# Left-over scatters placed behind the last weight split, and both halves of the last store issued by SP, in an attention, convolution and mixture-of-experts kernel

## The chip, the cores and the metric

The kernel runs on one core of one Trainium2 chip. The metric is the device time of one execution in microseconds (us). A TensorE, VectorE, ScalarE, GpSimd and SyncE instruction stands in the profile under PE (PEld for its weight loads), DVE, ACT, POOL and SP. The clock of TensorE has two levels, 2.4 and 1.2 GHz, which the profile shows as a granted clock of 1.0 and 0.5.

## The reference, cut to what matters

The inputs are q, k, v of 8 batches, 8 heads, 256 positions and 64 values a head, a gate of 8 x 256 x 512, a convolution of 15 taps for each of 512 channels, and 16 experts in 4 groups with weights of 512 x 1024 and 1024 x 512.

```
scores = q @ k.T / 8;  attn = softmax(scores);  x = attn @ v          # [8, 256, 512]
c = depthwise_conv(x * sigmoid(gate), conv_w);  x = x + c * sigmoid(c)
x = x.reshape(2048, 512)
g = argmax(x @ w_group);  e = argmax(x @ w_expert[g])                  # for each token
out = softmax(group logits)[g] * softmax(expert logits)[e] * (relu(x @ w1[g, e]) @ w2[g, e])
```

## The kernel before

**Stages.** The 2048 tokens are 16 tiles of 128, two for each of the 8 batches. Attention, convolution and routing run in four groups of two batches. The expert stage is split in two. The *dense* part (`dense`) takes each batch as a whole, finds the one expert that most of its 256 tokens chose, loads that expert's weights once and multiplies all 256 tokens with them; results of tokens that chose another expert are replaced afterwards or, for the loop at the end, recomputed. The *left-over* part (`leftover`) gathers tokens of the first six batches that chose another expert into three tiles of 32 rows, computes these with their own experts, and scatters the rows over the output with indirect DMAs that GpSimd issues (`spread`, which calls `scatter`, line 1297). A loop at the end (lines 1392 to 1404) handles further left-over tiles; its trip count is read on the chip, and with these inputs the profile shows the branch past it and no work of its body.

**Weights.** An expert's weights are 8 tiles of 128 x 1024 float32 (512 KB each): tiles 0 to 3 are the first layer, 4 to 7 the second. Every tile goes through `fetch` (SP issues its load, line 934) and `split`: ACT rounds the tile to `wh` (line 323, by way of `copy`), and then two halves of 512 columns give `wl` = raw - `wh` (line 957), most on POOL. For the last two batches all `wl` halves are on POOL. TensorE multiplies high with high, high with low and low with high parts, so it needs `wh` and `wl` of a tile: lines 984 for the first layer, 1019 to 1021 and, for the second 128 tokens of the last batch, 1010 to 1012 for the second layer. Two rings tie the steps together: 4 buffers `raw` (a fetch waits until POOL has split the tile four before it) and 4 pairs `wh`, `wl` (a cast waits until TensorE has used the tile four before it). I number the 64 tiles 0 to 63 over the batches; 56 to 63 belong to the last batch, `ms[-1]`. Hidden values go the same way: ACT makes `hh` (line 1032), DVE or, for tile 58, ACT and POOL make `hl` (lines 1041, 1038 and 1045).

**Order.** The order of instructions on each engine's queue is set when the program is built. A planner (`Flow`) runs all steps as coroutines over estimated durations: `yield run(engine, us)` queues a step, and of the steps that are ready on an engine the one with the lowest key goes next. Weight splits have key -1 and `spread` has key 50, so a scatter is placed where POOL has no other ready step in the plan; `fl.sc` keeps the three of them 2.3 us apart in the plan. `yield flag(f)` holds a step until another has set `f`. `m.st` are the flags of a batch's two stores, `m.w` those of its 8 split tiles. On the chip each queue then runs in that fixed order with semaphore waits. All scatters write the same rows, so each waits for the one before it to have landed.

**The end.** The last tile of 128 tokens is computed in two halves of 256 columns, and `half` scales each (DVE the first at line 1057, ACT the second at line 1055) and stores it (line 1060), the first from SP, the second from ACT. The 128 tokens before them are stored by `store` (line 1074).

Of the kernel before, what the change touches and what calls it, by code (L numbers as in the profile page):

```python
# [17 lines left out]
P = 128  # L18
# [70 lines left out]
class Flow:  # L89
# [169 lines left out]
    def run(self):  # L259
        while True:  # L260
            best = None
            for e, q in self.q.items():
                if q:
                    t = max(self.free[e], min(x[2] for x in q))
                    if best is None or t < best[0]:
                        best = t, e
            if best is None:
                return
            t, e = best
            if e == "PE":  # L270
                x = min((x for x in self.q[e] if x[2] <= t), key=lambda x: (x[0] + SW * (x[6] != self.shape), x[1]))
            else:
                x = min((x for x in self.q[e] if x[2] <= t), key=lambda x: x[:2])
            self.q[e].remove(x)
            k = x[4]
            k[2], k[3], k[4] = self.spot(e, t, x), e, e
            self.free[e] = k[2]
            self.step(k)
# [28 lines left out]
def flag(f):  # L307
    return "flag", f
# [7 lines left out]
def attn_conv_moe(ctx, tc, aQ, aG, cw, wr, wE, cst, out):  # L316
    nc = tc.nc
    v_, a_, g_, t_, s_ = nc.vector, nc.scalar, nc.gpsimd, nc.tensor, nc.sync

    on = dict(DVE=v_, POOL=g_, ACT=a_, SP=s_)  # L320
# [625 lines left out]
    ms = [M(b) for b in range(B)]  # L946
# [15 lines left out]
    def dense():  # L962
        for m in ms:
# [30 lines left out]
            for j in range(4):  # L994
# [5 lines left out]
                for t in range(2):  # L1000
                    sl = slice(t * P, (t + 1) * P)
                    if m.b == B - 1 and t == 1:
                        if j == 3:
                            yield get("y")
                            y = work.tile([P, DM], F32, name="y", bufs=2)
                        for h in range(2):
                            yield run("PE", 0.71)
                            c, yp = slice(h * S, h * S + S), ys[1 + h][:, 0:S]
                            for k in range(2):
                                t_.matmul(yp, hh[:, k, sl], w3h[:, k, c], start=j == 0 and k == 0, stop=False)  # L1010
                                t_.matmul(yp, hh[:, k, sl], w3l[:, k, c], start=False, stop=False)  # L1011
                                t_.matmul(yp, hl[:, k, sl], w3h[:, k, c], start=False, stop=j == 3 and k == 1)  # L1012
                            if j == 3:
                                fl.go(half(m, h, c, y, yp), -5, fl.now[2], "PE")
                        continue
                    for k in range(2):
                        if DC or k == 0:
                            yield run("PE", 0.705 if DC else 1.41)
                        t_.matmul(ys[t], hh[:, k, sl], w3h[:, k, :], start=j == 0 and k == 0, stop=False)  # L1019
                        t_.matmul(ys[t], hh[:, k, sl], w3l[:, k, :], start=False, stop=False)  # L1020
                        t_.matmul(ys[t], hl[:, k, sl], w3h[:, k, :], start=False, stop=j == 3 and k == 1)  # L1021
                    if j == 3:
                        fl.go(store(m, t, iy[t], ys[t]), -5, fl.now[2], "PE")
# [26 lines left out]
    def half(m, h, c, y, yp):  # L1050
        yield flag(gr[m.g].done)
        tt = 2 * m.b + 1
        yield run(("DVE", "ACT")[h], (0.35, 0.33)[h])
        if h:
            a_.activation(y[:, c], yp, AF.Copy, scale=rec[:, tt, 1:2])  # L1055
        else:
            v_.tensor_scalar(y[:, c], yp, rec[:, tt, 1:2], None, ALU.mult)
        w = ("SP", "ACT")[h]
        yield run(w, 0.43)
        on[w].dma_start(out=out[tt * P:(tt + 1) * P, c], in_=y[:, c])  # L1060

    def store(m, t, iy, yp):
        yield flag(gr[m.g].done)
# [232 lines left out]
    def scatter(o, n):  # L1296
        g_.indirect_dma_start(out=out_rows[0:n, :], out_offset=bass.IndirectOffsetOnAxis(ap=o.ix, axis=0),
                              in_=o.ys, in_offset=None, bounds_check=n - 1, oob_is_err=False)
# [51 lines left out]
    def leftover():  # L1350
        for s in range(NS):
            o = ls_[s]
            yield flag(ready[s])
            for h in range(2):
                for j in range(4 * h, 4 * h + 4):
                    yield flag(lraw[s][j])
                    fl.now[2] = max(fl.now[2], o.w[j][2])
                raw = [o.w[j][1] for j in range(4 * h, 4 * h + 4)]
                yield from (o.second(raw) if h else o.first(raw))
                for j in range(4 * h, 4 * h + 4):  # L1360
                    fl.put("gv", o.w[j][0])
            fl.go(spread(o), 50, fl.now[2])

    def spread(o):
        for m in ms[0:GB[GA]]:
            for f in m.st:
                yield flag(f)
        fl.now[2] = max(fl.now[2], fl.sc)
        yield run("POOL", 1.0)
        scatter(o, TA * P * NC)  # L1370
        fl.sc = fl.now[2] + 2.3
# [83 lines left out]
```

## Time and profile before

| | us |
|---|---|
| median of 3 runs | 352.19 |
| range of these runs | 350.96 to 352.76 |
| the profiled execution's own time | 351.07 |
| its span, first to last instruction | 349.3 |
| PE busy | 336.0 (96% of the span) |
| POOL busy | 286.0 (82%) |
| DVE busy | 256.2 (73%) |
| ACT busy | 239.5 (69%) |
| granted TensorE clock, mean | 0.989 |

A line of the timeline gives start and duration in us, the engine (SPq and ACTq: a DMA issued from that queue), the source line, the operation, what is written and read, and how many instructions; in brackets the engine's idle time ahead of it and what ended it. A matmul's end is modelled, so the idle time of PE is best read from one start to the next. A line of a window gives its length, the busy time of each engine with the number of instructions that start in it, the granted clock, the DMA engines' busy share and the GB/s they moved. The view of one source line gives durations as minimum, median and maximum in ns and the first and last start.

### The profile page before, as it was taken

The page shows a single profiled execution, that of the slowest core. Times are in us where ns is not written, and L with a number is a line of the kernel's source. Part 1 is how long each engine was busy: PE and PEld are TensorE (multiplying, and loading weights), DVE is VectorE, ACT ScalarE, POOL GpSimd, SP SyncE. Part 2 cuts the span into 40 slices and gives each one's busy share as a digit, 9 for nine tenths or more (in the row PEclk, how much of TensorE's full clock was granted, in tenths as well). Part 3 has the DMA queues.
Part 4 walks back from the last instruction along what each step waited for, and adds up shares of the span by engine and source line. Part 5 has one row for each costly group of instructions (what it writes and reads, how often), then busy time and mean ns, then how long its engine had stood idle before and what let it go on. Part 6 is the DMA issues. An engine that isn't in the chain of part 4 may idle for free. (4 is left out here: it accounts for less than half of the span.)

```text
span 349.3 us, 7977 instructions
## 1 busy us (share of the span) xinstructions
PE 336.0 (96%) x2749; PEld 272.9 (78%) x2749; DVE 256.2 (73%) x542; ACT 239.5 (69%) x546; POOL 286.0 (82%) x279
## 2 busy tenths in 40 slices
PE   8999999998999999999999999999999999999892
PEld 6766555567788789878877788899789788988872
DVE  1989997999999999999899888997994462101000
ACT  4999578969997797798988955365554535627211
POOL 0652477766999999999999989999899989993990
PEclk9999999999999999999999999999999999999897
DMA  7849896439955681568551545599999847556301
GB/s 252 292 142 270 233 261 213 150 137 341 350 180 202 190 293 62 213 239 269 206 192 68 175 139 224 187 340 391 407 408 410 326 149 266 190 188 176 121 3 66
DMA packets 29883, 77.89 MB, mean 223 GB/s; under 512 B 3230, under 2 KB 3798, under 8 KB 29840
## 3 DMA queue, kind: packets, MB, share of 16 engines
q1 hardware_dynamic: 27520, 73.31, 61.7%
q10 hardware_dynamic: 2160, 3.80, 2.9%
q8 instruction: 24, 0.39, 0.4%
q0 software_dynamic: 160, 0.23, 0.2%
q14 instruction: 19, 0.16, 0.1%
HBM read 65.50 MB, written 7.57 MB: 209 GB/s over the span
## 5 line engine op out<-in xcount | busy, mean ns | idle before, releaser
L957 POOL TENSOR_TENSOR wl<-raw,wh 128x512 fp32r<-128x512 f32 x121 | 156.0, 1318 | 7.6 <-ACT wh L323 3.8
L736 DVE SCALAR_TENSOR_TENSOR bk<-sl,cwq,bk 128x512 f32<-128x512 f32 x151 | 108.7, 747 | 2.2 <-ACT bk L723 0.5
L323 ACT CAST wh<-raw 128x1024 fp32r<-128x1024 f32 x64 | 67.1, 1054 | 29.8 <-DMA raw<-wE 13.0
L984 PE MATMUL bk<-sl,wh 128*128 128x256 f32 x512 | 74.0, 287 | 0.0
L984 PEld LDWEIGHTS bk<-sl,wh 128*128 128x128 f32 x512 | 65.8, 191 | 2.4 <-issue 1.6
L562 ACT ACTIVATE pr<-bk,nm 128x256 f32<-128x256 f32 x128 | 59.1, 487 | 9.8 <-DVE nm L557 9.7
L1019 PE MATMUL bk<-wh,hh 128*128 128x512 f32 x120 | 48.7, 406 | 0.0
L1020 PE MATMUL bk<-wl,hh 128*128 128x512 f32 x120 | 47.5, 396 | 0.7 <-POOL wl L957 0.7
L557 DVE TENSOR_REDUCE nm<-bk 128x2 f32<-128x512 f32 x64 | 40.3, 679 | 9.8 <-PE bk L528 9.7
L1021 PE MATMUL bk<-wh,hl 128*128 128x512 f32 x120 | 47.4, 395 | 0.0
L1041 DVE SCALAR_TENSOR_TENSOR hl<-bk,hh 128x512 fp32r<-128x512 f32 x16 | 11.0, 688 | 49.3 <-ACT hh L1032 42.6
L984 PE MATMUL bk<-sl,wl 128*128 128x256 f32 x256 | 41.4, 285 | 2.0 <-POOL wl L957 2.0
L984 PEld LDWEIGHTS bk<-sl,wl 128*128 128x128 f32 x256 | 35.5, 193 | 2.2 <-POOL wl L957 2.2
L569 PE MATMUL bk<-c_id,pr 128*128 128x128 f32 x256 | 34.9, 277 | 2.1 <-ACT pr L562 1.9
L1032 ACT ACTIVATE hh<-bk 128x512 fp32r<-128x512 f32 x32 | 19.2, 600 | 23.9 <-PE bk L984 16.5
L569 PEld LDWEIGHTS bk<-c_id,pr 128*128 128x128 f32 x256 | 28.0, 141 | 8.9 <-ACT pr L562 5.4
L528 PE MATMUL bk<-qk 64*128 64x256 f32 x256 | 34.3, 404 | 0.2
L548 PE MATMUL bk<-pT,gv 128*64 128x256 f32 x256 | 31.2, 386 | 0.0
L528 PEld LDWEIGHTS bk<-qk 64*128 64x128 f32 x256 | 24.6, 194 | 6.3 <-issue 1.9
L562 ACT ACTIVATION_READ_ACCUMULATOR pr<-bk,nm 128x1 f32 x128 | 28.1, 219 | 0.0
L1020 PEld LDWEIGHTS bk<-wl,hh 128*128 128x128 f32 x120 | 22.6, 188 | 5.6 <-POOL wl L957 1.1
L1021 PEld LDWEIGHTS bk<-wh,hl 128*128 128x128 f32 x120 | 22.6, 188 | 5.3
(176 smaller groups left out, 550.9 us busy)
## 6 DMA issues: line engine op xcount, KB each, us to landing
raw<-wE SPq DMA_DIRECT2D x64, 512.0 KB, 4.3
gv<-wE SPq DMA_DIRECT2D x24, 512.0 KB, 8.8
gv<-aG SPq DMA_DIRECT2D x16, 512.0 KB, 6.6
qk<-aQ SPq DMA_DIRECT2D x15, 512.0 KB, 5.6
out_dram<-y SPq DMA_DIRECT2D x9, 256.0 KB, 3.8
wh<-sl SPq DMA_DIRECT2D x8, 270.0 KB, 4.9
wl<-sl SPq DMA_DIRECT2D x8, 270.0 KB, 5.5
x_rows<-y ACTq DMA_DIRECT2D x8, 256.0 KB, 2.1
```

The source lines that it names most:

```text
L323: (a_.copy if e == "ACT" else on[e].tensor_copy)(o, i)
L528: t_.matmul(scs[hh][:, qt, :], t[sl, i, qt * P:(qt + 1) * P], t[sl, i, 256:512], start=True, stop=True)
L548: t_.matmul(u.a[64 * hh:64 * hh + 64, i, :], u.vt[:, i, kt, hh, :], pTs[hh][1][:, kt, :], start=kt == 0, stop=kt == 1)
L557: v_.reduce_max(nm[:, hh, :], sc, axis=AX.X, negate=True)
L562: a_.activation(pr[:, qt, :], sc[:, qt, :], AF.Exp, bias=nm[:, hh, qt:qt + 1], scale=1.0, accum_out=u.sm[:, i, qt, hh, 0:1])
L569: t_.transpose(tp[:, kt, qt * P:(qt + 1) * P], pr[:, qt, kt * P:(kt + 1) * P], ident)
L736: v_.scalar_tensor_tensor(acc if k == KT - 1 else ac, x, w, acc if k == m and m > 1 else ac, ALU.mult, ALU.add)
L957: on[e].tensor_tensor(wl[:, sl], raw[:, sl], wh[:, sl].bitcast(F32), ALU.subtract)
L984: t_.matmul(hp[:, f, :], ww[:, f, c, :], x, start=k == 0, stop=k == 11)
L1019: t_.matmul(ys[t], hh[:, k, sl], w3h[:, k, :], start=j == 0 and k == 0, stop=False)
L1020: t_.matmul(ys[t], hh[:, k, sl], w3l[:, k, :], start=False, stop=False)
L1021: t_.matmul(ys[t], hl[:, k, sl], w3h[:, k, :], start=False, stop=j == 3 and k == 1)
```

## The change

Two edits. `half` issues the store of both halves from SP, where the second was issued from ACT. `spread`, which places one scatter of left-over rows, waits for the eight splits of the last batch's weights in addition to the stores of the first six batches, so that all three scatters stand behind the last split on POOL's queue.

```diff
@@ half
             a_.activation(y[:, c], yp, AF.Copy, scale=rec[:, tt, 1:2])
         else:
             v_.tensor_scalar(y[:, c], yp, rec[:, tt, 1:2], None, ALU.mult)
-        w = ("SP", "ACT")[h]
-        yield run(w, 0.43)
-        on[w].dma_start(out=out[tt * P:(tt + 1) * P, c], in_=y[:, c])
+        yield run("SP", 0.43)
+        s_.dma_start(out=out[tt * P:(tt + 1) * P, c], in_=y[:, c])
@@ spread
         for m in ms[0:GB[GA]]:
             for f in m.st:
                 yield flag(f)
+        for f in ms[-1].w:
+            yield flag(f)
         fl.now[2] = max(fl.now[2], fl.sc)
         yield run("POOL", 1.0)
         scatter(o, TA * P * NC)
```

## Rows read from the trace of the kernel before

**Rows 1.** Chain that ended last, its two ends: start us, duration us, what

```profile
336.79 1.25 POOL wl L957
...
342.99 0.47 ACT y L1055
```

**Rows 2.** Timeline of PE, last batch: first layer, then second layer

```profile
315.62 1.11 PE L984 MATMUL bk<-sl,wh 128*128 128x256 f32 x8
...
318.46 1.11 PE L984 MATMUL bk<-sl,wh 128*128 128x256 f32 x8
...
321.30 1.11 PE L984 MATMUL bk<-sl,wh 128*128 128x256 f32 x8
324.43 1.22 PE L984 MATMUL bk<-sl,wl 128*128 128x256 f32 x4 [2.02 <-POOL wl L957]
...
330.79 0.40 PE L1019 MATMUL bk<-wh,hh 128*128 128x512 f32 x1
...
336.32 0.39 PE L1019 MATMUL bk<-wh,hh 128*128 128x512 f32 x1
...
337.01 0.40 PE L1019 MATMUL bk<-wh,hh 128*128 128x512 f32 x1
338.08 0.50 PE L1020 MATMUL bk<-wl,hh 128*128 128x512 f32 x1 [0.67 <-POOL wl L957]
338.42 0.39 PE L1021 MATMUL bk<-wh,hl 128*128 128x512 f32 x1
...
342.67 0.28 PE L1012 MATMUL bk<-wh,hl 128*128 128x256 f32 x1
```

**Rows 3.** Windows: length; PE, PEld, DVE, ACT, POOL; clock; DMA share; GB/s

```profile
324.40:327.90 3.50, 3.48 (x16) 3.48 (x17) 0.00 (x0) 0.00 (x0) 3.50 (x3) 0.51 0.02 9
```

**Rows 4.** Timeline of POOL: the three scatters

```profile
315.33 1.03 POOL L1297 DMA_INDIRECT out_dram<-ys,ixs  x1 [0.16 <-issue]
322.10 0.98 POOL L1297 DMA_INDIRECT out_dram<-ys,ixs  x1 [5.73 <-DMA out_dram<-ys,ixs]
...
339.43 0.99 POOL L1297 DMA_INDIRECT out_dram<-ys,ixs  x1 [0.16 <-issue]
```

**Rows 5.** Windows of POOL's outage and of the stretch behind it, columns as before

```profile
315.33:323.08 7.75, 7.07 (x58) 6.77 (x57) 1.38 (x2) 5.43 (x7) 2.02 (x3) 1.00 0.61 167
323.08:339.28 16.20, 14.18 (x88) 12.99 (x89) 0.69 (x1) 3.80 (x5) 16.19 (x13) 0.89 0.21 67
```

**Rows 6.** Line 1297, the three scatters from issue to landing

```profile
DMA to landing us min/median/max: 2.1/2.1/6.5
```

**Rows 7.** Timeline of ACT: casts of tiles 58 to 62 and the `tm` of tile 58

```profile
315.00 1.04 ACT L323 CAST wh<-raw 128x1024 fp32r<-128x1024 f32 x1
...
317.09 2.19 ACT L323 CAST wh<-raw 128x1024 fp32r<-128x1024 f32 x2 [0.47 <-ACT y L1069]
...
322.00 1.04 ACT L323 CAST wh<-raw 128x1024 fp32r<-128x1024 f32 x1
...
328.64 0.59 ACT L1038 ACTIVATE tm<-bk 128x512 f32<-128x512 f32 x1
330.00 1.06 ACT L323 CAST wh<-raw 128x1024 fp32r<-128x1024 f32 x1 [0.77 <-DMA raw<-wE]
```

**Rows 8.** Timeline of SP: the fetches of tiles 62 and 63

```profile
326.84 1.56 SPq L934 DMA_DIRECT2D raw<-wE  x2
```

**Rows 9.** Timeline, line 1060: the stores of the last two halves

```profile
342.82 0.35 SPq L1060 DMA_DIRECT2D out_dram<-y  x1
...
343.49 0.34 ACTq L1060 DMA_DIRECT2D out_dram<-y  x1
```

**Rows 10.** Line 1060: the last half from issue to landing

```profile
DMA to landing us min/median/max: 3.2/3.2/3.2
```

**Rows 11.** Line 1393, branch past the loop on TensorE's queue, from 343 us

```profile
L1393 PEldq COMPARE_BRANCH  x1: 3792/3792/3792, 343.1 to 343.1; - x1
```

**Rows 12.** Line 1074, two stores of 256 KB beside the first scatter: issue to landing

```profile
DMA to landing us min/median/max: 5.7/5.7/5.7
```

## The prediction

> **What bounds the kernel now.** I read the page's busy shares first (PE 96%), then the chain of waits, then the timelines of PE and POOL over the last batch, because both edits lie there. The chain is short [rows 1]: it runs from ACT's scaling of the last half back through TensorE's second layer to one weight split on POOL that ends at 336.79 + 1.25 = 338.04 us. So the end of the kernel hangs on TensorE, and TensorE in turn hung on POOL shortly before. The timeline of PE shows two places where it waited for `wl` [rows 2]: at 324.43 (tile 58) and at 338.08 (tile 62). Around the first the granted clock fell to the lower level: the mean is 0.51 over 324.40 to 327.90, right after TensorE had stood idle [rows 3]. The reason stands in POOL's timeline: scatter one is issued at 315.33, scatter two waits 5.73 us for the first to land and is issued at 322.10 [rows 4]. From 315.33 to 323.08 POOL thus does no split (its 2.02 busy us are the two scatters), and from 323.08 to 339.28 it runs 13 operations without a gap, 16.20 / 13 = 1.246 us each [rows 5]: it is catching up until the last split. Scatter three already stands behind the last split.
>
> **Edit 1, what it takes away on TensorE.** Tiles 56 and 57 take 318.46 - 315.62 = 321.30 - 318.46 = 2.84 us each at full clock. Tiles 58 and 59 at that pace would end at 321.30 + 2 x 2.84 = 326.98; the second layer begins at 330.79 [rows 2]. That is 3.81 us, of which some 2.1 are the stall and the rest matmuls at the low clock [rows 2, 3]. In the second layer three starts take 337.01 - 336.32 = 0.69, so 0.23 each; the matmul due at 337.24 starts at 338.08 (0.84 lost) and the one after it 0.34 later (0.11 lost) [rows 2]. Sum: 3.81 + 0.95 = **4.76 us**, if POOL no longer holds TensorE up.
>
> **Does POOL keep up without the two scatters?** Up to 315.33 its queue is the same. ACT's casts of tiles 58 to 61 end at 316.04, about 318.2, 319.28 and 323.04 [rows 7], and none of them waited for POOL's outage. I take the order of halves that the stretch behind the outage has (two tiles interleaved), which is the less favourable one: half 58a at 316.1, 59a when cast 59 is done at 318.2, then at 1.246 us each 58b, 59b, 60a, 60b up to 324.4, 61a to 325.7, the `hl` of tile 58 to 326.9 (its `tm` at 328.64 - 3.81 = 324.8 to 325.4 [rows 7]), 61b to 328.2. Fetch 62 needs 58b, done at 320.7, so it leaves then instead of at 326.84 [rows 8]. Its landing was seen by ACT at 330.00, 3.2 us after issue [rows 7, 8]; with 6.5 (the scatter's worst [rows 6], taken as a bound) it lands at 327.2 and its cast ends at 328.3, when POOL gets to it. Tile 63's cast has to wait until TensorE is through with tile 59 at 326.98 and ends at 328.1. So 62a, 63a, 62b, 63b run from 328.2 to 333.2, with 62b ready at 331.9. TensorE wants it at 326.98 + (336.32 - 330.79) + 0.92 = 333.43 [rows 2]. The slack is 1.5 us, some 5 us for tile 58 (wanted at 322.4, ready at 317.4). TensorE is then the bound throughout, and its last matmul ends at 342.67 + 0.28 - 4.76 = 338.19 instead of 342.95 [rows 2].
>
> **Edit 1, what it adds.** Three scatters in a row behind the last split, each waiting for the one before. Third and second scatter landed in 2.1 us and the first in 6.5 [rows 6]; from a landing (315.33 + 6.5 = 321.83) to the next issue pass 0.27 us [rows 4]. The DMA engines were 0.61 busy in the window around the first, and 0.21 in the one behind [rows 5]; at the end no fetch is left, so I take 2.1: 333.2 + 0.16 (idle before an issue [rows 4]) + 3 x 2.1 + 2 x 0.27 = 340.2. Bounds: 3 x 2.1 to 3 x 6.5, an end between 340.2 and 353.4. Behind the scatters only POOL's part of the closing waits is queued; no engine needs POOL for data any more. What covers them is the end of the program: TensorE's branch past the loop takes 3.79 us from 343.1 to 346.9 [rows 11], and the last half lands at 343.49 + 3.2 = 346.7 [rows 9, 10]; from there to the span's end at 349.3 pass 2.4 us. Both move 4.76 us forward, to 342.1. The scatters land 1.9 us before that, so they cost nothing; without that cover each us of them is a us of the kernel.
>
> The Trainium skill, "DMA: Bandwidth & Descriptors", section "Latency and other measured facts", puts the fixed cost of a DMA down mostly to the memory's latency, small at light load and up to 2 us at high load. By that the 2.1 us scatters are the quiet case and three of them stay covered; the 6.5 us one in a busy window agrees with it in direction only.
>
> **Edit 2.** SP has finished issuing the first half at 342.82 + 0.35 = 343.17, before ACT ends the second at 342.99 + 0.47 = 343.46 [rows 1, 9], so SP issues it no later than ACT did (343.49). A gain is excluded, since the branch ends at 346.9 and the landing at 346.7: an earlier landing is hidden. A loss is bounded by the landing of two stores beside the first scatter, 5.7 instead of 3.2 [rows 10, 12]: 343.49 + 5.7 = 349.2, 2.3 us past the branch. I take zero: the nearest row is the last half itself.
>
> **The rivals.**
> *Part of the gain is given back* (chance 0.09). One of the three scatters takes 6.5 us: the chain ends at 340.2 + 4.4 = 344.6, 2.5 past the cover, and 4.76 - 2.5 = 2.3 us remain, 349.9. A plan that puts the last splits some 3 us later than I do gives about the same. Against it: tile 62's slack of 1.5 us and the empty DMA engines.
> *The scatters slow the last stores* (0.05). The third scatter now runs beside them, as the first did beside two stores of 256 KB that took 5.7 us [rows 12]. The end moves back 2.3 us: gain 2.4, 349.8. Against it: those stores shared the DMA engines with a weight fetch too.
> In the same section, the Trainium skill says that two of the 16 DMA engines are usually slower and gives GpSimd's descriptor rings as a best guess; by it stores beside scatters would land late, which is this rival. No row here tells it from plain load.
> *Nothing that can be told from no change* (0.08). The outage belongs to this one execution, because scatter one is usually as quick as the others: the outage would be 4.4 us shorter and 4.76 - 4.4 = 0.4 us is left, 351.8. Against it: the profiled execution (351.07) is among the shortest, where it should be the longest. Or the plan orders the last batch otherwise and TensorE finds another wait.
> *Slower* (0.04). The serial chain of three becomes the end. From 333.3 on, each us of mean landing counts three times. It breaks even when the chain ends at the old 346.9, at a mean of (346.9 - 333.3 - 0.5) / 3 = 4.4 us, and is slower by over 0.5% from 4.9. At 6.5 each it ends at 353.4, 6.5 past the old point: 358.7. For it: one of three was that slow. Against it: that one shared the DMA engines with a fetch.
>
> **How the numbers follow.** The profiled execution's own time is 351.07 for a span of 349.3, so 1.8 us lie around the span and stay. It is 1.1 us under the median of the runs; I subtract from the median: 352.19 - 4.76 = **347.4** (346.3 by the profiled execution). Forecast 0.74, and its own range is 345.9 to 348.8: the spread of the runs before is 1.8 us, and TensorE's sum can be off by some half a us. The two rivals that give a part back lie at 349.8 and 349.9, so the range goes to 350.0. A change under 0.5% (1.8 us) can't be told from none here. Faster by more than that: 0.74 + 0.09 + 0.05 = 0.88; within it 0.08; slower 0.04.
>
> **What would show it.** Right: no wait for `wl` on PE in the last batch, clock 1.0 up to the last matmul, the second layer some 3.8 us earlier; POOL without a gap over 1 us between 318 and 333, then three scatters about 2.4 us apart, the last one landed before the branch past the loop is over; both halves' stores on SP. Wrong: a wait of ACT for a fetch or of TensorE for `wl` in tiles 60 to 63, a landing of a scatter above 4 us, or a last store that lands after the branch is over.

## The result, and the profile after

| | before | after |
|---|---|---|
| median of 3 runs, us | 352.19 | 347.71 |
| range of these runs | 350.96 to 352.76 | 346.21 to 348.57 |
| the profiled execution's own time | 351.07 | 347.71 |
| its span | 349.3 | 345.9 |

The ratio is 0.9866, with an interval of 0.9817 to 0.9915. The changed kernel is 4.5 us faster, at 347.7 us; forecast were 4.76 us and 347.4 us. Run again, the ratio is 0.9843 (0.9814 to 0.9872). Some executions of a kernel are over 1.5% longer than its fastest: the ratios leave them out, and the trace of edit 2 alone is of such an execution and stands in no table below.

The two profiled executions differ by only 3.4 us. The difference to the 4.70 us below lies ahead of the edits: the first matmul of tile 56 starts at 315.62 before [rows 2] and at 316.95 after, 1.33 us later. A second execution of the kernel before has it at 317.30, so this is spread between executions. The mean clock of the execution after is again 0.989, but for another reason: it fell once, at 10.9 us of the span, and was at a mean of 0.51 until 14.3. From here on I therefore use two lengths that do not contain it: the **stage**, from the first matmul of tile 56 to the end of the span, and the **tail**, from the start of the last matmul to the end of the span. Before: stage 349.31 - 315.62 = 33.69, tail 349.3 - 342.67 = 6.63 [rows 2]. After: stage 345.94 - 316.95 = 28.99, tail 6.69. The stage lost **4.70 us**; 4.76 was forecast.

First the chain that ended last, after (start, duration, what); it answers to [rows 1].

```profile
317.11 11.37 PE bk L984 x96
...
339.41 0.13 PE bk L1012
339.56 0.47 ACT y L1055
```

In [rows 1] a weight split on POOL stood in the last 13 us of the chain. Now the whole first layer of the last batch is one unbroken stretch of 96 TensorE instructions, and no split comes behind it.

The timeline of PE after, last batch, answers to [rows 2].

```profile
316.95 1.11 PE L984 MATMUL bk<-sl,wh 128*128 128x256 f32 x8
...
319.79 1.11 PE L984 MATMUL bk<-sl,wh 128*128 128x256 f32 x8
...
322.63 1.11 PE L984 MATMUL bk<-sl,wh 128*128 128x256 f32 x8
...
325.47 1.11 PE L984 MATMUL bk<-sl,wh 128*128 128x256 f32 x8
...
328.31 0.40 PE L1019 MATMUL bk<-wh,hh 128*128 128x512 f32 x1
...
339.25 0.28 PE L1012 MATMUL bk<-wh,hl 128*128 128x256 f32 x1
```

All four tiles of the first layer take 2.84 us each, and no line has a wait in brackets. The second layer begins 328.31 - 316.95 = 11.36 us after tile 56, where it was 330.79 - 315.62 = 15.17: 3.81 earlier. The last matmul comes 22.30 after tile 56 where it was 27.05: 4.75 earlier.

Windows after, with the columns of [rows 3, 5] (length; PE, PEld, DVE, ACT, POOL; clock; DMA share; GB/s): the first layer, then the second.

```profile
316.95:328.31 11.36, 11.36 (x97) 11.36 (x96) 1.39 (x2) 7.42 (x11) 10.86 (x9) 1.00 0.69 203
328.31:339.50 11.19, 11.19 (x74) 9.94 (x72) 1.18 (x2) 2.20 (x3) 8.11 (x8) 1.00 0.02 4
```

PE is busy in all of both, at a granted clock of 1.00, and POOL for 10.86 of 11.36 us in the first. POOL's timeline shows why; it answers to [rows 4, 5].

```profile
317.45 10.05 POOL L957 TENSOR_TENSOR wl<-raw,wh 128x512 fp32r<-128x512 f32 x8 [0.95 <-ACT wh L323]
327.44 1.31 POOL L1045 TENSOR_TENSOR hl<-tm,hh 128x512 fp32r<-128x512 f32 x1
328.68 5.06 POOL L957 TENSOR_TENSOR wl<-raw,wh 128x512 fp32r<-128x512 f32 x4
333.89 1.03 POOL L1296 DMA_INDIRECT out_dram<-ys,ixs  x1
336.43 0.98 POOL L1296 DMA_INDIRECT out_dram<-ys,ixs  x1 [1.51 <-DMA out_dram<-ys,ixs]
338.83 0.97 POOL L1296 DMA_INDIRECT out_dram<-ys,ixs  x1 [1.43 <-DMA out_dram<-ys,ixs]
```

The outage of 7.75 us in [rows 5] is gone: eight splits, `hl` and four splits run one behind the other, the last ends at 333.74, and then come three scatters.

The last lines answer to [rows 7], ACT's casts of tiles 61 and 63,

```profile
323.68 1.05 ACT L323 CAST wh<-raw 128x1024 fp32r<-128x1024 f32 x1 [0.25 <-DMA raw<-wE]
...
328.17 1.05 ACT L323 CAST wh<-raw 128x1024 fp32r<-128x1024 f32 x1 [0.48 <-PE bk L984]
```

to [rows 8, 9], SP's queue with the fetches of tiles 62 and 63 and now both halves' stores,

```profile
320.01 4.09 SPq L934 DMA_DIRECT2D raw<-wE  x2
338.91 0.35 SPq L1073 DMA_DIRECT2D out_dram<-y  x1
339.39 1.00 SPq L1059 DMA_DIRECT2D out_dram<-y  x2
```

to [rows 6], line 1296, the three scatters from issue to landing,

```profile
DMA to landing us min/median/max: 2.1/2.3/4.4
```

to [rows 10], line 1059, the last half,

```profile
DMA to landing us min/median/max: 3.3/3.3/3.3
```

and to [rows 11], line 1394, the branch past the loop on TensorE's queue (ns):

```profile
L1394 PEldq COMPARE_BRANCH  x1: 3852/3852/3852, 339.7 to 339.7; - x1
```

The branch ends at 339.71 + 3.85 = 343.56, the last half lands at 340.06 + 3.34 = 343.40, and the third scatter lands at 338.83 + 4.39 = 343.22. All three end within 0.34 us of one another, 2.4 us ahead of the end of the span.

### The profile page after: what moved, and what is told of

Same layout as the page of the kernel before. It is cut to its first block, busy times and chain, and to the rows that moved or that the text cites. A ratio compares the mean times of both kernels' runs of the same rounds, so it can differ in the third digit from the quotient of the medians.

```text
span 345.9 us, 7977 instructions
## 1 busy us (share of the span) xinstructions
PE 333.7 (96%) x2749; PEld 271.3 (78%) x2749; DVE 256.7 (74%) x542; ACT 239.9 (69%) x546; POOL 285.8 (83%) x279
## 4 chain that ended last, share of the span: by engine, by line
PE 62%; DVE 10%; ACT 8%; POOL 7%; DMA 6%; issue 3%; SPq 0%; POOLq 0%; ACTq 0%; DVEq 0%
PE bk L984 19%; PE bk L1019 6%; PE bk L1020 6%; PE bk L1021 6%; PE bk L569 6%; PE bk L528 6%; PE bk L548 5%; ACT pr L562 5%; DVE bk L736 5%; POOL wl L957 4%; DMA qk<-aQ 4%; PE bk L688 3%; DMA raw<-wE 3%; DVE nm L557 2%; PE bk L808 1%
## 5 line engine op out<-in xcount | busy, mean ns | idle before, releaser
L984 PE MATMUL bk<-sl,wh 128*128 128x256 f32 x512 | 73.2, 285 | 0.0
L984 PEld LDWEIGHTS bk<-sl,wh 128*128 128x128 f32 x512 | 64.9, 189 | 2.4 <-issue 1.6
L984 PE MATMUL bk<-sl,wl 128*128 128x256 f32 x256 | 40.5, 280 | 0.0
L528 PE MATMUL bk<-qk 64*128 64x256 f32 x256 | 33.7, 400 | 1.8 <-DVE qk L480 1.7
L984 PEld LDWEIGHTS bk<-sl,wl 128*128 128x128 f32 x256 | 34.7, 188 | 0.0
L528 PEld LDWEIGHTS bk<-qk 64*128 64x128 f32 x256 | 23.9, 190 | 7.9 <-DVE qk L480 2.0
L1019 PEld LDWEIGHTS bk<-wh,hh 128*128 128x128 f32 x120 | 22.6, 188 | 4.9 <-issue 0.4
```

Of the source, the lines that this page charges most:

```text
L528: t_.matmul(scs[hh][:, qt, :], t[sl, i, qt * P:(qt + 1) * P], t[sl, i, 256:512], start=True, stop=True)
L984: t_.matmul(hp[:, f, :], ww[:, f, c, :], x, start=k == 0, stop=k == 11)
```

## The experiments

Theory: POOL's outage in the last batch, made by the second scatter waiting in POOL's queue for the first to land, is the whole cost; edit 1 takes it away; edit 2 does nothing; the three scatters at the end are covered. Rivals: the outage belonged to one execution; part of the cost was the low clock and would go with it alone; the scatters are only just covered, or cost something.

The times of single executions carry the spread ahead of tile 56, so there I go by stage and tail. What each traced execution gave, in us (the first column is its own time):

| kernel | time | tile 56 at | 2nd layer after it | stage | tail | branch |
|---|---|---|---|---|---|---|
| before | 351.07 | 315.62 | 15.17 | 33.69 | 6.63 | 3.79 |
| before again | 352.81 | 317.30 | 14.70 | 33.75 | 6.64 | 3.80 |
| after | 347.71 | 316.95 | 11.36 | 28.99 | 6.69 | 3.85 |
| after again | 347.68 | 316.53 | 11.36 | 29.27 | 6.98 | 4.14 |
| scatters alone | 347.01 | 315.94 | 11.36 | 29.30 | 7.00 | 4.16 |
| one scatter early | 348.54 | 317.50 | 11.36 | 29.27 | 6.97 | 4.14 |
| scatters spread out | 350.90 | 319.87 | 11.36 | 29.25 | 6.96 | 4.12 |
| wait filled | 352.92 | 316.19 | 15.52 | 34.90 | 6.94 | 4.08 |
| fourth scatter | 351.58 | 317.39 | 11.36 | 32.36 | 10.06 | 3.80 |
| no loop | 345.78 | 317.64 | 11.36 | 26.27 | 3.98 | none |
| short loop | 346.97 | 316.17 | 11.36 | 29.04 | 6.85 | 0.39 |

With the whole loop in the program the branch takes 3.8 or 4.1 to 4.2 us, whatever else is changed; 28.99 and 29.27, the same kernel twice, differ by just that.

**The kernel before again.** No edit.

> The kernel before once more, for its trace. Theory (the outage of POOL is a property of the kernel): the second scatter waits for the first again, POOL does no weight split for 5 to 8 us at the start of the last batch, TensorE waits for a split of tile 58 or 62, and from the start of tile 56 to the end of the span pass 32.5 to 34.5 us (33.7 in the first trace). Rival (the landing of 6.5 us belonged to that one execution): the first scatter lands in 2 to 3 us, the outage is under 4 us and the same stretch takes 29 to 30.5 us.

Measured: 352.81 us. POOL's timeline in the last batch:

```profile
317.01 1.03 POOL L1297 DMA_INDIRECT out_dram<-ys,ixs  x1 [0.16 <-issue]
323.79 0.98 POOL L1297 DMA_INDIRECT out_dram<-ys,ixs  x1 [5.74 <-DMA out_dram<-ys,ixs]
```

The waits of PE there (total, times, longest):

```profile
PE bk L984 <- POOL wl L957: 2.8, 2, 2.0
PE bk L1020 <- POOL wl L957: 0.9, 2, 0.7
```

The window of the stretch behind the outage:

```profile
324.77:340.92 16.15, 13.19 (x88) 11.49 (x89) 0.69 (x1) 3.68 (x5) 16.15 (x13) 1.00 0.22 67
```

The outage is there again, with the first scatter landing in 323.79 - 0.27 - 317.01 = 6.5 us as in [rows 6]: it belongs to the kernel and not to one execution. The window is to be read beside the second of [rows 5]. The clock is 1.00 here, where it was 0.89, so in this execution it did not fall, although PE stood idle 2.03 us at the same place. In exchange PE waited a second time in the first layer (2.8 us in all, where it was 2.0). The stage is 33.75, 0.06 from the other. What did not change is POOL: 13 operations without a gap after the outage, the last split 23.62 us after tile 56 (23.65 before), and the last matmul 344.40 - 340.92 = 3.48 us behind its end (342.67 - 339.27 = 3.40). In both executions TensorE follows POOL, whatever its clock does on the way.

**The clock by itself.** The kernel before, with 36 products of zeros into a spare bank where TensorE waits for the second half of tile 58.

```diff
+                            if m.b == B - 1 and n == 2 and f == 0 and k == 8:
+                                ib2 = yield take("bk", 1, "lo")
+                                yield run("PE", 0.1)
+                                fill(ib2, 36)
+                                fl.back("bk", ib2, "lo")
```

> The kernel before, with 36 matmuls of zeros (bfloat16, 128 columns, into a free bank) put on TensorE at the place of its wait for tile 58, so that it is busy there. Theory (POOL's lateness sets the end, the low clock behind the wait costs nothing of its own): TensorE runs at the full clock, waits longer at tile 62 instead, and from the start of tile 56 to the end of the span still pass 33.4 to 34.1 us. Rival (the sum of the prediction read as two costs, wait and clock): 1.7 us less, 32.0 us.

Measured: the timeline of PE at the wait and of POOL's first two scatters:

```profile
322.82 2.18 PE L407 MATMUL bk<-wz 128*128 128x128 bf16 x36
...
316.39 1.03 POOL L1302 DMA_INDIRECT out_dram<-ys,ixs  x1 [0.15 <-issue]
323.49 0.98 POOL L1302 DMA_INDIRECT out_dram<-ys,ixs  x1 [6.06 <-DMA out_dram<-ys,ixs]
```

The windows of the outage and of the stretch behind it:

```profile
316.39:324.47 8.08, 8.08 (x86) 8.03 (x85) 1.38 (x2) 4.97 (x7) 2.02 (x3) 1.00 0.56 165
324.47:340.68 16.21, 13.75 (x98) 11.87 (x96) 0.69 (x1) 3.78 (x6) 16.20 (x13) 1.00 0.20 67
```

TensorE is busy all through the outage and the clock stays at 1.00 in both windows, and the stage is 34.90, not shorter than 33.7. The last matmul again comes 344.15 - 340.68 = 3.47 us behind the last split. The stage is 1.2 us longer than before, which none of the expectations had. Of that, the outage began 0.20 us after tile 56 where it had begun 0.29 ahead of it, it lasted 8.08 instead of 7.75 us, and the branch took 0.29 more: 0.49 + 0.33 + 0.29 = 1.11. The lateness was also expected to move on to tile 62, and hardly did: beyond the filler TensorE waited 1.6 us in the first layer and 0.9 in the second, where the second execution without the filler had 0.9, too. Were the low clock a cost of its own, some 1.7 us (3.81 less the stall of 2.1) would be gone here. That rival falls.

**Each edit alone.** Both are shown as what is taken back from the changed kernel: edit 1 alone keeps the second half's store on ACT, edit 2 alone leaves out the new wait of `spread`. The first:

```diff
-        yield run("SP", 0.43)
-        s_.dma_start(out=out[tt * P:(tt + 1) * P, c], in_=y[:, c])
+        w = ("SP", "ACT")[h]
+        yield run(w, 0.43)
+        on[w].dma_start(out=out[tt * P:(tt + 1) * P, c], in_=y[:, c])
```

> Edit 1 alone: the three scatters behind the last split, the second half still stored from ACT. Theory: all of the gain is here; 28.6 to 29.4 us from the start of tile 56 to the end of the span (28.95 with both edits, 33.68 before), a time 4 to 5 us under the kernel before. Rival (the two edits only pay together, because scatters and stores meet at the end): a smaller gain, under 3.5 us.

and the second:

```diff
-        for f in ms[-1].w:
-            yield flag(f)
```

> Edit 2 alone: the second half stored from SP, the scatters where they were. Theory: no difference, within 0.3% of the kernel before, the same wait of TensorE for splits in the last batch, and the span ends some 6.3 us after the last matmul as before. Rival (a queue of its own made the last half land earlier): 0.5 to 2 us slower; other rival (ACT's issue held something up): 0.5 us faster.

Both edits together, on the same chip:

> The changed kernel once more. Theory: no wait of TensorE for splits in the last batch, 28.6 to 29.4 us from the start of tile 56 to the end of the span, a time 4 to 5 us under the kernel before; what runs of the same kernel differ by lies ahead of the last batch. Rival (part of the gain is the luck of one execution): a stretch of over 30 us, a gain under 3 us.

| | median, us | ratio to before | interval |
|---|---|---|---|
| edit 1 alone | 347.41 | 0.9871 | 0.9833 to 0.9908 |
| edit 2 alone | 352.15 | 0.9988 | 0.9959 to 1.0017 |
| both | 347.17 | 0.9843 | 0.9814 to 0.9872 |

The gain is edit 1's. Edit 2 makes no difference that can be measured, and with edit 1 the stage is 29.30 without it and 29.27 with it. The Trainium skill, "DMA: Bandwidth & Descriptors", section "Issuing engines are not separate DMA queues", says that issuing from several engines saves only the time that the issuing takes; the runs agree, since SP issued the second half at 340.06, 0.03 us after ACT had finished it (339.56 + 0.47), as ACT had done before (343.49 after 343.46).

**Is it a scatter among the splits that costs, or the wait of the second for the first?** The first scatter may go early again, the other two stay at the end.

```diff
-        for f in ms[-1].w:
+        for f in ms[-1].w if o is not ls_[0] else ():
             yield flag(f)
```

> The changed kernel, with the first scatter back at its old place and the second and third behind the last split. Theory (what cost POOL its time is the second scatter's wait for the first, not a scatter as such): the first scatter again takes 6 to 7 us to land, nobody waits for it, POOL is held 1.0 us, TensorE waits for no split in the last batch, and from the start of tile 56 to the end of the span pass 28.7 to 29.4 us. Rival (any scatter ahead of the last splits makes them late): TensorE waits for tile 58 or 62, the stretch takes 30 us or more.

Measured, in POOL's timeline:

```profile
317.24 1.03 POOL L1296 DMA_INDIRECT out_dram<-ys,ixs  x1
318.30 10.02 POOL L957 TENSOR_TENSOR wl<-raw,wh 128x512 fp32r<-128x512 f32 x8
```

The first scatter from issue to landing:

```profile
DMA to landing us min/median/max: 6.1/6.1/6.1
```

The scatter is nearly as slow as before, 6.1 us for 6.5. But POOL goes on to the next split 1.06 us after the issue, because nothing behind the scatter in its queue needs it landed. PE has no wait for `wl`, and the stage is 29.27, that of the changed kernel. A slow scatter among the splits takes one microsecond of POOL, most of it out of the 0.95 us in which POOL waits for a cast in the changed kernel: the last split ends 17.05 us after tile 56 for 16.79. The second scatter waiting behind it was the cost.

That all scatters write the same rows, as the description of the kernel before has it, is not quite so. Each tile has its own tokens and so its own rows; but line 1297 names the same range of `out_rows` for all three, and by that range the second waits for the first. Whether it could be issued without this wait was not tried.

**The scatters early but far apart.** No wait for the splits; each scatter is placed at the first chance, the next one only 9 us later in the plan.

```diff
+            self.out = Flag()
...
-        for f in ms[-1].w:
-            yield flag(f)
+        if o is not ls_[0]:
+            yield flag(ls_[ls_.index(o) - 1].out)
         fl.now[2] = max(fl.now[2], fl.sc)
-        yield run("POOL", 1.0)
+        yield run("POOL", 1.0, -2)
         scatter(o, TA * P * NC)
-        fl.sc = fl.now[2] + 2.3
+        fl.sc = fl.now[2] + 9.0
+        fl.set(o.out)
```

> The scatters ahead of the last batch's end: as soon as the stores of the first six batches are issued and then some 9 us apart among the splits. Theory: each takes 1.0 to 1.2 us of POOL and none waits for the one before it; POOL's slack of 1.5 us and more covers that, 28.7 to 29.6 us from the start of tile 56 to the end, no long wait of TensorE for splits. Rival (3 us more work on POOL reach TensorE in the last two batches): waits of TensorE for splits of 1 to 3 us in all.

Measured: 350.9 us beside 350.46 for the kernel before. POOL's timeline at the first scatter:

```profile
297.82 1.03 POOL L1297 DMA_INDIRECT out_dram<-ys,ixs  x1 [4.11 <-DMA out_dram<-y]
```

The waits of PE from 290 us on:

```profile
PE bk L1020 <- POOL wl L957: 1.3, 2, 0.7
PE bk L984 <- POOL wl L957: 1.1, 1, 1.1
```

The last batch is as good as in the changed kernel (stage 29.25; the third scatter, issued 0.33 us after tile 56, took 6.5 us with no one behind it, the two earlier ones 2.2 each). But the first scatter has to wait for the stores of the first six batches, whose rows it overwrites, and now it does so at the head of POOL's queue for 4.11 us, one batch earlier. PE then waits 1.1 + 1.3 us there, and tile 56 starts at 319.87, 2.2 to 4.3 us later than in the other kernels of the table. The outage had moved, not gone. The waits of 1 to 3 us that the rival named came, behind this wait of POOL; what the scatters' own 3 us of work added to them was not separated.

**How much cover is there at the end?** The changed kernel with the last scatter issued twice.

```diff
         scatter(o, TA * P * NC)
+        if o is ls_[-1]:
+            yield run("POOL", 1.0)
+            scatter(o, TA * P * NC)
```

> The changed kernel with the third scatter issued twice, so four in a row behind the last split; the same rows are written twice. Theory from the trace of after (the third landing comes 0.3 us ahead of TensorE's branch): the cover is used up, a fourth scatter adds most of its 2.4 us, 31.0 to 31.7 us from the start of tile 56 to the end against 29.0. By the sum of the prediction (1.9 us of cover left): 0.5 us more, 29.5.

Measured: POOL's last two scatters in its timeline:

```profile
339.75 0.97 POOL L1296 DMA_INDIRECT out_dram<-ys,ixs  x1 [1.42 <-DMA out_dram<-ys,ixs]
343.88 0.97 POOL L1296 DMA_INDIRECT out_dram<-ys,ixs  x1 [3.16 <-DMA out_dram<-ys,ixs]
```

The four scatters from issue to landing:

```profile
DMA to landing us min/median/max: 2.1/3.0/3.9
```

The stage is 32.36, 3.4 us longer than that of the changed kernel, with all matmuls where they were (22.30 after tile 56). By the cover of 1.9 us that I had predicted, a fourth scatter would have cost 2.1 + 0.27 - 1.9 = 0.5. The third lands at 343.62 and the branch ends at 340.16 + 3.80 = 343.96: 0.34 us, as in the changed kernel. The fourth, landing in 3.4 us at 347.24, then is the end, and 2.5 us behind it the span is over. That is also more than the 31.0 to 31.7 expected for the stage, which counted 2.4 us for it. The third scatter, too, is slow again: 3.9 us.

**What makes the third scatter slow?** At the end three things run at once: the branch, the last half's store and the third scatter. The changed kernel without the loop for further left-over tiles (lines 1392 to 1404 of the kernel before; with these inputs its body does no work) has no branch.

```diff
-    v_.tensor_scalar(pos, pos, float(NS * LT), None, ALU.subtract)
-    n = nc.values_load(eidi[0:1, 0:1], min_val=NS, max_val=NT // LT + 2 * NE)
-    with tc.For_i(NS, n, 1) as i:
...
-        scatter(o, NT * NC)
```

> The changed kernel without the loop for further left-over tiles, whose body doesn't run with these inputs; this part of the computation is left out. Theory (TensorE's branch past the loop takes 3.8 us and the fetch of instructions behind it holds up one DMA engine): without it the third scatter lands in under 3 us and the last half in under 2.2 us, and from the start of the last matmul to the end of the span pass 3.5 to 4.8 us instead of 6.7. Rival (the late pieces are late by the stores or the scatter themselves): the landings stay at 4.4 and 3.3 us and the same stretch takes 5.5 us or more.

Measured: the third scatter from issue to landing,

```profile
DMA to landing us min/median/max: 2.5/2.5/2.5
```

and the last half:

```profile
DMA to landing us min/median/max: 1.7/1.7/1.7
```

The two DMAs are the same as in the changed kernel and land in 2.5 and 1.7 us instead of 4.4 and 3.3. The stage is 26.27: the last landing comes at 342.63, 24.99 after tile 56, where the branch had ended 26.61 after it, and from there to the span's end pass 1.3 us instead of 2.4: 1.6 + 1.1 = 2.7 us.

**The branch or what it fetches?** The loop stays, but its gather on TensorE has 20 matmuls instead of 64, so that the branch jumps over less code.

```diff
-        yield run("PE", 0.09 * ntt)
...
-            for c in range(NC):
-                t_.matmul(ip[c * LT:(c + 1) * LT, 0:2], sel[:, t, :], rec[:, t, :], start=t == 0, stop=t == ntt - 1)
+            t_.matmul(ip[0:LT, 32:34], sel[:, t, :], rec[:, t, :], start=t == 0, stop=t == ntt - 1)
+        swa = small.tile([P, 2], F32, name="swl")
+        v_.tensor_copy(swa[0:LT], ip[0:LT, 32:34])
+        for c in range(NC):
+            t_.matmul(ip[c * LT:(c + 1) * LT, 0:2], ident[0:LT, 0:LT], swa[0:LT], start=True, stop=True)
```

> The changed kernel with a shorter body of the closing loop on TensorE: 20 matmuls instead of 64 find a tile's rows (16 into 32 partitions, 4 that copy these to the other three groups of partitions). The body doesn't run with these inputs. Theory (the branch past the body is dear because of how much code it leaps over): the branch takes under 1 us instead of 3.8 to 4.2, the last matmul is followed by some 4.5 to 5.5 us instead of 6.7 to 7.0, and the third scatter lands in 2.1 to 2.7 us. Rival (any branch past a body of this size waits for instructions): no difference, 6.7 to 7.0 us.

Measured: the longest branch on TensorE's queue and the wait behind it (ns):

```profile
L1396 PEldq COMPARE_BRANCH  x1: 393/393/393, 338.8 to 338.8; - x1
L1396 PEldq EVENT_SEMAPHORE  x1: 3322/3322/3322, 339.3 to 339.3; - x1
```

The landing of the third scatter,

```profile
DMA to landing us min/median/max: 4.5/4.5/4.5
```

and of the last half:

```profile
DMA to landing us min/median/max: 3.6/3.6/3.6
```

The branch takes 0.39 us instead of 3.85, and the end hardly moves: tail 6.85, a miss of the expectation that it would get shorter by more than a microsecond, and the third scatter's 4.5 us miss the 2.1 to 2.7. TensorE now waits 3.32 us in the closing waits instead, because scatter and store still land late, at 342.56 and 342.76. So two things end together: the branch, and two DMAs that are slow at this time. Shortening the branch alone leaves the other.

The trace also holds the records of single DMA packets. A store or scatter lands in 16 pieces. Of the changed kernel's last half 15 pieces have landed by 341.84 and one at 343.4; of its third scatter 15 by 341.57 and one at 343.22. At this time an instruction packet of 16 KB (queue q8) is in transfer, from 341.21 to 342.17, and the late piece of the store starts at 342.18. The same stands in the kernel before (packet to 345.52, late piece from 345.50) and with the short loop (both 341.38); in two traces, after again and fourth scatter, the piece starts 0.3 us later, behind a scatter's packet that itself starts when the instruction packet ends. Without the loop there is no such packet at the end and no late piece. So the late piece very likely waits behind this packet; no run moved the packet alone, so it is not shown.

For the long branch the Trainium skill, "Runtime: NRT & Kernel Launch", section "Instruction fetch mechanics", gives a mechanism: a taken branch whose target is not yet loaded has to fetch the target's page before the engine goes on. 3.85 us over the long body and 0.39 over the shorter one agree with it in direction; which code was loaded at that moment no run here shows.

Of the kernels that still hold all of the computation none is shown to beat the changed one; the one that is shorter has lost its loop, which other inputs need.

## Why the prediction was right

**The bound.** That the end hung on TensorE and TensorE on one of POOL's splits was right, and the outage as its cause was, too: in a second execution of the kernel before it came back, and the stage with it (33.69 and 33.75); a kernel with one early scatter and no wait behind it has no outage and the changed kernel's stage.

**Edit 1, the sum.** 3.81 us of the first layer were taken away exactly (15.17 to 11.36), 0.94 of the 0.95 of the second layer, and in all the stage is 4.70 us shorter for 4.76 forecast. One term was **taken apart wrongly**: "2.1 are the stall and the rest matmuls at the low clock". It describes that trace, but the two are not two costs. In the second execution of the kernel before, the clock did not fall in the last batch, and the same loss (27.10 - 22.30 = 4.80 us up to the last matmul, 4.75 in the first) lay around waits instead (2.8 and 0.9 us for 2.0 and 0.7). The sum held since it was read from starts on PE, against the pace of the undisturbed tiles, and not added up from waits. The cost was POOL's lateness, and the clock only decided in which form TensorE paid.

**POOL keeps up.** Right, with a detail better than assumed. The assumed order took two tiles interleaved, with the last split 17.6 us after tile 56; it ended 16.8 after it (333.74 - 316.95). Fetch 62 left 3.1 us after tile 56 instead of 5.1. The largest gap of POOL is 0.95 us, for a cast, ahead of the first of these splits. One of the signs named for wrong did come, without consequence: ACT waited 0.25 us for the fetch of tile 61, and POOL ran on.

**The three scatters at the end.** Right in the result, **wrong in size**. The step that failed is "at the end no fetch is left, so I take 2.1". There is no weight fetch, but the third scatter met the branch's stretch and took 4.4 us (4.4 in after again, 4.6 with the scatters alone, 4.5 with the short loop). With 2.3, 2.1 and 4.4 the chain from the first issue to the last landing took 343.22 - 333.89 = 9.3 us, not the 6.8 of the prediction, and the cover left is 0.34 us, not 1.9. The 2.1 us were right for the second scatter and nearly so for the first (2.3). The 4.4 us were another of the signs I had named for wrong (a landing above 4 us). It cost nothing only because it stayed inside the cover, and that was luck: the chain was 2.5 us longer than calculated, more than the 1.9 us, and fitted only because it began 0.8 us earlier than calculated (333.89 - 316.95 = 16.94 us after tile 56 for 333.36 - 315.62 = 17.74). The fourth scatter shows what lies beyond, 3.4 us for one.

**The end.** The branch and the last half set the end again, tail 6.63 and 6.69. Both do, within 0.16 us of each other. The short loop showed that shortening the branch alone gains nothing; the other way round was not run.

**Edit 2.** Zero, as forecast: 0.9988 (0.9959 to 1.0017).

**The rivals.** Part given back, by a 6.5 us scatter at the end or a late plan: none of it. Slow last stores beside the scatters: the last half took 3.3 us for 3.2 (3.7 in after again, and landed at 343.31, under a branch that ended at 343.4). The 5.7 us of [rows 12] are one landing, that of ACT's store; the line gives none for SP's. No change, because the outage was one execution's: the second execution shows it with the same 6.5 us. Slower through the chain of three: that needed a mean landing over 4.4 us; the mean is (2.3 + 2.1 + 4.4) / 3 = 2.9.

## What to carry to other kernels

When a DMA in an engine's queue must wait for an earlier one to land, put the pair where nothing behind them in that queue is needed: one scatter among the splits took 1 us of POOL, a second one behind it 5.7 us of waiting and 1 us of its own, and placing them from one batch earlier on only moved the outage there, to the wait for the stores. Price a stall from the starts on the bounding engine against its undisturbed pace, since in another execution the same lateness may appear as waits instead of a low clock. Before leaning on cover at the end of a program, add one more of the covered thing and measure: here 1.9 us of calculated cover was 0.3.

## What the runs showed of the hardware

**A clock that fell in one execution and not in another.** After TensorE had stood idle for 2.02 us the granted clock was at a mean of 0.51 for 3.5 us in the kernel before [rows 3]; after 2.03 us at the same place in a second execution of the same kernel it was 1.00 throughout.

**A slow stretch of the DMA engines early in the last batch.** Windows of 2 us, before and then after, with the columns of the windows above:

```profile
316.00:318.00 2.00, 2.00 (x20) 2.00 (x19) 0.00 (x0) 1.53 (x3) 0.36 (x1) 1.00 0.96 115
```

```profile
317.50:319.50 2.00, 2.00 (x19) 2.00 (x18) 0.00 (x0) 1.52 (x2) 2.00 (x2) 1.00 1.05 102
```

The engines are fully busy (0.96 and 1.05) and move only 115 and 102 GB/s, where the first layer as a whole had 203 GB/s at 0.69. In the second there is no scatter at this time at all. The fetch of tile 61, issued at 316.53 after, was there only just before ACT's cast of it at 323.68, some 7 us later. So the early scatter met a stretch that is slow without it, too. That this is why it took 6.5 us is not shown: in the kernel with the scatters spread out the one issued at 320.20 took 6.5 us as well, while the 2 us from 320.4 on moved 212 GB/s at 0.66. What the traces do show is the place: at the start of the last batch a scatter took 6.1 to 6.8 us in five executions of four kernels, and 2.2 us at the two earlier places of the spread-out kernel, the second of them at a DMA share of 0.44. What makes the place slow is open.

**The end of a program is not a quiet place for DMAs.** The same scatter took 2.5 us and the same store 1.7 us without the loop, 4.4 and 3.3 with it, though there was no weight fetch in either. With the loop, one of the 16 pieces of each lands some 1.6 us after the rest, beside an instruction packet of 16 KB that takes about 1 us.
